# Pooled attention and an affine MLP: the order of batch 0's heads, one load for half of w_ch1, and batch 1's v summed by four tokens a partition

## The chip, the cores and the metric

The kernel runs on one core of a Trainium2 chip. A core has five engines with a program each: TensorE (PE, the matrix unit; PEld is its weight load), VectorE (DVE), ScalarE (ACT), GpSimd (POOL) and SyncE (SP). They wait for each other by semaphores. PE reads SBUF and writes PSUM; the DMA engines move data between the chip's memory and SBUF. The metric is the device time of one execution, in microseconds (us).

## The reference

q, k and v are 8 batches of 8 heads of 576 tokens by 64 numbers. Keys and values are averaged over groups of 8 tokens, so each head has 72 pooled ones. Attention's output, put together to 8 x 576 x 512, goes through an MLP with a token mix and a channel mix:

```python
k_p = k.reshape(B, H, Sp, pool, D).mean(axis=3)          # pool = 8, Sp = 72
v_p = v.reshape(B, H, Sp, pool, D).mean(axis=3)
attn = softmax(scale * q @ k_p^T)
x = (attn @ v_p), heads side by side                     # 8 x 576 x 512
a1 = alpha1 * x + beta1
u = x + lam * einsum('ts,bsd->btd', w_tok, a1)
a2 = alpha2 * u + beta2
out = u + lam * (maximum(a2 @ w_ch1, 0) @ w_ch2)         # 512 -> 2048 -> 512
```

## The kernel before

All work is written out by hand in one order; each engine runs its own instructions in that order, so an instruction that waits holds up everything behind it on its engine. The tokens of two batches make 9 chunks of 128 (4 of each, and one that holds the last 64 of both). Four chunks are a block, and there are nine blocks. Three pieces follow each other.

**The prologue** (lines 189 to 748) loads batch 0, makes constants, runs batch 0's attention and token mix and starts the MLP of block 0. Per head or head group:

- `att_F` (L367, L372) transposes q on PE and copies it from PSUM; `att_K` (L404, L410, L420) pools the keys of four heads by matmuls against a pooling matrix; `att_S` (L454, L457, L459) makes a head's scores and ACT takes their exponential into `ET`; `first_V` (L430, L432, L435) pools four heads' values on PE, four matmuls with `pool_v` (128 tokens) and two with `pool_vr` (32), and DVE copies them into `vp1_pool`, one copy for two heads.
- `att_AV` (L518, L522) multiplies `ET` by the values; DVE takes the reciprocal of the sums and scales (L524, L526). `att_X` (L540) and `rest_X` (L533) multiply by lam and alpha1 into `xs`, on DVE or GpSimd. `spread_al1` (L285, L286) spreads alpha1 over the partitions, 256 columns a call.
- `setup_wtok` (L300, L303) transposes one of five strips of w_tok, PE and an ACT copy; `setup_rowsum` (L312, L314) sums it over its tokens, for beta1. `setup_bias` (L348, L350) makes a quarter of the hidden bias from beta2 and the matching quarter of w_ch1.
- `mix_T` (L572, L576, L579) is the token mix of a chunk, five matmuls of 512 columns; `mix_uT` (L593, L595) transposes its result into `u_fm`.
- `keep_warm` (L563) is a matmul of 512 columns whose result nobody reads.

**The loads** that matter are issued by GpSimd, and so move in one queue in the order of issue: batch 0, w_tok, `load_w1(0)` and `load_w1(1)` (the four w_ch1 quarters are tiles of their own, `w1_of` picks the 128 columns of hidden chunk j), q and k of batch 1, `load_w1(2)`, v of batch 1 (`load_v`, 72 partitions, one group of 8 tokens a partition), `load_w1(3)`, and four quarters of w_ch2.

**The blocks** (lines 796 to 830): block n runs 64 `mlp_A` matmuls (L609, ACT's bias and relu L614) and 64 `mlp_B` matmuls (L643, DVE L649 and L650), with the attention and mix of batch n+1 in between. Every item has a place, a number; the list is sorted by it, and `mlp_A(n, j)` has place j, `mlp_B` 16 to 31. For batch 1 (`first`), q is transposed on PE, and `att_V` (L442, L444) sums a pair of heads' v over 8 tokens by three DVE additions. `att_S4` (L474, L481) makes four heads' scores, whose exponentials (L503) are placed one by one. Tiles named `gp` share six PSUM buffers, those named `ch` two.

Of the kernel before, what the change touches and what calls it, by code (L numbers as in the profile page):

```python
# [7 lines left out]
FP = mybir.dt.float32  # L8
F16 = mybir.dt.float16
BF = mybir.dt.bfloat16  # L10
AF = mybir.ActivationFunctionType
ALU = mybir.AluOpType
AX = mybir.AxisListType

P = 128
SPG = 72
# [7 lines left out]
def kernel(  # L24
# [18 lines left out]
    nc = tc.nc  # L43
# [21 lines left out]
    st1 = {}  # L65
# [30 lines left out]
    def load_v16(b, parts=(0, 1, 2)):  # L96
# [9 lines left out]
        for part in parts:  # L106
# [4 lines left out]
            else:  # L111
# [2 lines left out]
                    out=main[:, 4 * u:4 * u + 4].rearrange("p h c d -> p h (c d)"),  # L114
                    in_=rows(v, b, u))

    def load_rem(b, queue=nc.sync, behind=None):

        raw = work.tile([P, 2, 2, 2, D], FP, tag="rem_raw", bufs=2, name="rem_raw")
        if behind is not None:  # L120
            behind.memset(raw[:, :, :, 0, 0:1], 0.0)
        for i, src in enumerate((q, k)):
            for h in range(2):
                (nc.scalar if h and not b else queue).dma_start(
                    out=raw[:, i, h].rearrange("p c d -> p (c d)"),
                    in_=src[b, h::2, 512:576, :].rearrange("a (i c) d -> i a (c d)", c=2))
        st1[b]["rem_raw"] = raw

    def load_v(b, u, parts=(0, 1), behind=None, queue=nc.sync):

        if parts[0] != 1:
            st1[b]["v"][u] = work.tile([SPG, 4, 8, D], FP, tag="v_u", bufs=2, name="v_u")
        v_u = st1[b]["v"][u]
        if behind is not None:
            for rows_ in (slice(0, 64), slice(64, SPG)):
                behind.memset(v_u[rows_, 0, 0, 0:1], 0.0)  # L136
        for part in parts:
            g0, g1 = ((0, 64), (64, SPG), (0, SPG))[part]
            queue.dma_start(
                out=v_u[g0:g1].rearrange("g h p d -> g h (p d)"),  # L140
                in_=v[b, 4 * u:4 * u + 4, 8 * g0:8 * g1].rearrange("h (g p) d -> g h (p d)", p=8))

# [113 lines left out]
    def bias_row(i):  # L256
        p0 = 64 - 64 * i
        nc.vector.tensor_tensor(out=xs_pool[i][p0:p0 + 1, 4, :], in0=vecs[p0:p0 + 1, 1],
                                in1=vecs[p0:p0 + 1, 0], op=ALU.mult)
# [21 lines left out]
    def spread_al1(half):  # L281

        ps = gp("ps_bc")[:, 0:256]
        cols = slice(256 * half, 256 * half + 256)
        nc.tensor.matmul(out=ps, lhsT=ones_row, rhs=vecs[0:1, 2, cols])  # L285
        nc.vector.tensor_tensor(out=lamal_bc[:, cols], in0=lam_bc[:, cols], in1=ps, op=ALU.mult)  # L286
# [32 lines left out]
        nc.sync.dma_start(out=wtT[0:1, 5, 0:S], in_=wtT[64:65, 4, 0:S])  # L319


    w1 = [const.tile([P, 4, 512], BF, tag=f"w1_{g}", name=f"w1_{g}") for g in range(4)]
    w2 = [const.tile([P, 4, DM], BF, tag=f"w2_{g}", name=f"w2_{g}") for g in range(4)]

    def w1_of(cc, j):
        return w1[j // 4].rearrange("p c (m i) -> p c i m", i=4)[:, cc, j % 4, :]

    def load_w1(g):
        nc.gpsimd.dma_start(
            out=w1[g],  # L330
            in_=moe_w_ch1[:, 512 * g:512 * g + 512].rearrange("(cc p) j -> p cc j", p=P))

    def load_w2(g):
        nc.gpsimd.dma_start(
# [88 lines left out]
    def first_V(b, u, copy=nc.vector.tensor_copy):  # L423

        main, rest = st1[b]["v"]
        ps_v = gp("ps_v")
        vp = ps_v[0:SPG, 0:4 * D]
        heads = slice(4 * u, 4 * u + 4)
        for c in range(4):
            nc.tensor.matmul(out=vp, lhsT=pool_v, rhs=main[:, heads, c], start=(c == 0), stop=False)  # L430
        for c in range(2):
            nc.tensor.matmul(out=vp, lhsT=pool_vr, rhs=rest[:, heads, c], start=False,  # L432
                             stop=(c == 1))
        for r in range(2):
            copy(out=vp1_pool[2 * u + r][:, :, 0:64],  # L435
                 in_=vp[:, 128 * r:128 * r + 128].rearrange("p (h d) -> p h d", h=2))
# [122 lines left out]
    def keep_warm(count):  # L559

        ps = psB.tile([P, DM], FP, tag="ch", bufs=2, name="ps_warm")
        for _ in range(count):
            nc.tensor.matmul(out=ps, lhsT=warm[:, 0:P], rhs=warm)  # L563
# [93 lines left out]


    new_batch(1)
    for g in range(2):  # L660
        load_w1(g)
    load_q_bf(1, 0)
    load_q_bf(1, 1)
    for u in range(2):
# [10 lines left out]
    keep_warm(1)  # L675
    double_k(0)
    att_K(0, 0, None)
    bias_row(0)
    keep_warm(1)
    att_S(0, 0)  # L680
    att_S(0, 1)
    first_V(0, 0)
# [1 line left out]
    double_k(1)  # L684
    att_AV(0, 0)
    att_S(0, 3)
    keep_warm(1)
    att_K(0, 1, None)
    att_AV(0, 1)
    att_F(0, 2)  # L690
    att_F(0, 3, nc.vector.tensor_copy)
    spread_al1(0)
    att_X(0, 0, 2, nc.gpsimd, False)
    att_S(0, 4)
    att_AV(0, 2)
    spread_al1(1)
    att_S(0, 5)
    keep_warm(1)
    first_V(0, 1)
    keep_warm(1)  # L700
    att_AV(0, 3)
    att_X(0, 2, 4, nc.gpsimd, False)
    load_al2(nc.vector)
    att_S(0, 6)
    keep_warm(1)
    setup_vectors()
    att_AV(0, 4)
    keep_warm(2)
    att_S(0, 7)
    keep_warm(1)  # L710
    att_AV(0, 5)
    load_rem(1, behind=nc.vector)
    att_X(0, 4, 6, nc.gpsimd, False)
    setup_wtok(0, nc.scalar.copy)
    setup_wtok(1, nc.scalar.copy)
    att_AV(0, 6)
    setup_rowsum(0)
    att_AV(0, 7)
    setup_wtok(2, nc.scalar.copy)
    setup_rowsum(1)  # L720
    setup_bias(0)
    setup_wtok(3, nc.scalar.copy)
    att_X(0, 6, 8, nc.vector, False)
    rest_X(0, 0, H)
    load_w1(2)
    for u in range(2):
        load_v(1, u, (2,), queue=nc.gpsimd)
    mix_T(0, 0, nc.gpsimd)
    setup_rowsum(2)
    mix_T(0, 1)  # L730
    setup_rowsum(3)
    load_w1(3)
    load_w2(0)
    mix_T(0, 2, nc.gpsimd)
    load_w2(1)
    mix_uT((0, 0))
    mix_T(0, 3)
    mix_uT((0, 1))
    setup_wtok(4, nc.scalar.copy)
    setup_bias(1)  # L740
    mlp_A(0, 0, 0, 256)
    mlp_A(0, 1, 0, 256)
    mix_uT((0, 2))
    mlp_A(0, 2, 0, 256)
    mix_uT((0, 3))
    mlp_A(0, 3, 0, 256)
# [4 lines left out]
    def attention(b):  # L751


        first = b == 1
        todo = []
        if first:
            for hp in range(4):
                todo.append((2.6 + 0.9 * hp, lambda hp=hp: att_F(b, hp)))
            todo.append((3.5, lambda: cast_rem(b, nc.gpsimd)))
            for u in range(2):  # L760
                todo.append((3.65 + 0.1 * u, lambda u=u: load_w2(2 + u)))
            todo.append((7.4, lambda: att_Frem(b, nc.scalar.copy)))
        if b < B - 1:
            at = 28.5 if first else 10.0
            todo.append((at, lambda: att_F(b + 1, 0)))
            todo.append((at + 0.1, lambda: att_F(b + 1, 2)))
            at = 26.6 if first else 25.5
            todo.append((at - 1.0, lambda: cast_rem(b + 1, nc.gpsimd)))
            todo.append((at, lambda: att_Frem(b + 1)))
        for u in range(2):  # L770
            todo.append((3.6 + 0.1 * u if first else -0.9 + 1.2 * u,
                         lambda u=u: sum_k(b, u, nc.gpsimd)))
            todo.append((6.4 + 2.2 * u if first else 4.1 + 2.0 * u,
                         lambda u=u: att_K(b, u, nc.vector.tensor_copy)))
        for u in range(2):
            at = (9.0 if first else 6.3, 13.6)[u]
            todo.append((at, lambda u=u: att_S4(b, u)))
            for k, dt in enumerate((0.1, 0.1, 0.1, 0.7, 1.7, 1.75) if u else (0.1, 0.1, 0.1, 1.1, 2.1, 3.1)):
                todo.append((at + dt, lambda u=u, k=k: st1[b]["exp", u](k)))
            for i, dt in enumerate((2.9, 3.4, 4.6, 5.1) if u else (5.7, 6.2, 2.9, 3.4)):  # L780
                h = 4 * u + i
                todo.append((at + dt, lambda h=h: att_AV(b, h)))
                if i % 2:
                    eng = nc.gpsimd if h == 5 else nc.vector
                    todo.append((at + dt + 0.1, lambda h=h, eng=eng: att_X(b, h - 1, h + 1, eng)))
        for i, hp in enumerate((1, 0, 2, 3) if first else range(4)):
            todo.append(((6.6, 8.7, 10.0, 12.6)[i] if first else 0.2 + 2.0 * hp, lambda hp=hp: att_V(b, hp)))
        for c in range(5):
            at = 21.0 + 1.3 * c
            if c < 4 or b % 2:  # L790
                todo.append((at, lambda c=c: mix_T(b, c)))
                key = (b, c) if c < 4 else (b - 1, 4)
                todo.append((at + 1.8, lambda key=key: mix_uT(key)))
        return todo

    for n in range(NBLK):
# [2 lines left out]
            todo.append((j, lambda j=j: mlp_A(n, j)))  # L799
        for m in range(4):  # L800
            for part in range(4):
                at = 16 + 4 * m + part
                todo.append((at, lambda m=m, part=part: mlp_B(n, m, part)))
        if n == 0:
            todo.append((4.5, lambda: bias_row(1)))
# [55 lines left out]
```

The softmax here doesn't subtract the row's maximum and nothing guards it: scores larger than these inputs give would overflow.

## Time and profile before

| what | value |
|---|---|
| time, median of 3 | 346.69 us (346.46 to 346.94) |
| span of the profiled run | 343.8 us |
| PE busy in 0 to 20 us | 17.95 us |
| PE busy in 20 to 40 us | 19.16 us |
| PE busy in 40 to 60 us | 19.93 us |
| mlp_A L609: busy, mean of one | 133.3 us, 374 ns |
| mlp_B L643: busy, mean of one | 130.9 us, 379 ns |
| keep_warm L563: count, mean of one | 16, 505 ns |
| att_V's first additions L442, 72x512 and 72x256 | 681 ns, 420 ns |
| first_V's copies L435 | 282 ns |

Matmuls overlap in the pipeline: a mean of 379 ns for 512 columns is from start to end of one, while two starts are some 0.22 us apart. Busy time is the union. So a PE that is busy all the time isn't necessarily at its peak; what it waits for shows as idle with a releaser, and in the chain of work that ended last. A DMA issue (DMA_DIRECT2D) on GpSimd is short; the transfer behind it ends when it has landed, which the view of DMA issues lists as the time from issue to landing.

### The profile page before, as it was taken

The numbers are of one execution on the slowest core, as the hardware profiler recorded it, in microseconds if no ns is written. First come the engines' busy times: TensorE is split into PE (matmuls) and PEld (weight loads), VectorE is DVE, ScalarE is ACT, GpSimd is POOL, SyncE is SP. The second block draws the span as 40 slices with busy tenths as digits, with TensorE's granted clock in tenths as the row PEclk, the third lists the DMA queues.
The fourth block names the chain that finished last, engine by engine and source line by source line (L and its number), as shares of the span: only waits on it lengthen the run. The fifth ranks groups of instructions, "written<-read, shape, count | busy, mean of one in ns | idle before, by whom it ended". The sixth has DMA issues, their size and how long they took to land.

```text
span 343.8 us, 5902 instructions
## 1 busy us (share of the span) xinstructions
PE 337.1 (98%) x2221; PEld 177.4 (52%) x2221; DVE 224.7 (65%) x476; ACT 146.9 (43%) x277; POOL 90.2 (26%) x105
## 2 busy tenths in 40 slices
PE   8999999999999999999999999999999999999995
PEld 3667654455445544555445544554455445545544
DVE  6664579985787667866867598768675881037511
ACT  3655980068205830385028500880089006604700
POOL 8768507201144012701170117002600200000000
PEclk9999999999999999999999999999999999999999
DMA  8999999968678907794479437982810132011012
GB/s 123 184 222 287 215 202 248 188 139 130 161 210 172 194 2 192 150 225 54 129 200 213 65 110 179 204 131 63 241 41 1 48 76 78 0 61 62 2 54 68
DMA packets 66654, 45.77 MB, mean 133 GB/s; under 512 B 34457, under 2 KB 57373, under 8 KB 66626
## 3 DMA queue, kind: packets, MB, share of 16 engines
q1 hardware_dynamic: 51716, 32.73, 40.2%
q0 software_dynamic: 14448, 12.40, 22.6%
q8 instruction: 17, 0.28, 0.3%
q10 hardware_dynamic: 462, 0.27, 0.3%
q14 instruction: 11, 0.09, 0.1%
HBM read 38.30 MB, written 9.44 MB: 139 GB/s over the span
## 4 chain that ended last, share of the span: by engine, by line
PE 95%; DMA 2%; ACT 1%; DVE 1%; issue 0%; ACTq 0%; POOLq 0%
PE ps_h L609 36%; PE ps_ch L643 35%; PE ps_tok L572 11%; PE ps_s L474 2%; PE ps_av L518 2%; DMA q_bf<-in_q_dram 2%; PE ps_ch L632 1%; PE ps_kp L404 1%; PE ps_warm L563 1%; PE ps_q L367 1%; PE ps_sc L454 1%; PE ps_r L481 1%; PE ps_av L522 1%; PE ps_bias L348 0%; PE ps_bc L285 0%
## 5 line engine op out<-in xcount | busy, mean ns | idle before, releaser
L614 ACT ACTIVATE Hj<-ps_h,bias_cols 128x512 bf16<-128x512 f32 x144 | 98.3, 689 | 164.4 <-PE ps_h L609 163.1
L609 PE MATMUL ps_h<-u_fm,w 128*128 128x512 bf16 (+1 forms) x592 | 133.3, 374 | 0.2 <-ACT u_fm L595 0.2
L643 PE MATMUL ps_ch<-w,Hj 128*128 128x512 bf16 x560 | 130.9, 379 | 0.0
L609 PEld LDWEIGHTS <-w 128*128 128x128 bf16 x592 | 63.8, 114 | 51.7 <-issue 3.0
L643 PEld LDWEIGHTS <-Hj 128*128 128x128 bf16 x560 | 52.9, 98 | 61.6 <-issue 1.6
L572 PE MATMUL ps_tok<-xs,wtT 128*128 128x512 bf16 (+3 forms) x200 | 44.9, 380 | 0.3 <-DVE xs L540 0.3
L649 DVE TENSOR_TENSOR ps_ch<-lam_bc,ps_ch 128x512 f32<-128x512 f32 x32 | 22.2, 693 | 33.3 <-PE ps_ch L643 33.0
L540 POOL TENSOR_TENSOR xs<-x_tm,lamal_bc 128x512 bf16<-128x512 f32 x10 | 12.7, 1269 | 112.5 <-DVE x_tm L526 110.4
L576 DVE TENSOR_TENSOR u_sb<-x_tm,ps_tok 128x512 f32<-128x512 f32 (+1 forms) x40 | 27.4, 684 | 10.6 <-PE ps_tok L572 10.5
L524 DVE RECIPROCAL rec<-ps_av 128x5 f32<-128x5 f32 x64 | 12.2, 191 | 32.5 <-PE ps_av L522 32.4
L526 DVE TENSOR_TENSOR x_tm<-ps_av,rec 128x320 f32<-128x320 f32 x64 | 31.5, 492 | 2.7
L650 DVE TENSOR_TENSOR u_sb<-u_sb,ps_ch 128x512 f32<-128x512 f32 x35 | 24.0, 687 | 13.6 <-PE ps_ch L643 12.5
L503 ACT ACTIVATE ET<-ps_s 72x512 f16<-72x512 f32 x56 | 32.3, 592 | 0.0
L442 DVE TENSOR_TENSOR v_u<-v_u 72x512 f32<-72x512 f32 (+1 forms) x56 | 30.8, 550 | 1.0
L572 PEld LDWEIGHTS <-wtT 128*128 128x128 bf16 (+3 forms) x200 | 17.4, 100 | 21.3 <-issue 1.7
L579 DVE TENSOR_TENSOR u_bf<-u_sb,al_bc 128x512 bf16<-128x512 f32 x34 | 26.7, 785 | 1.7 <-DMA u_fm<-u_bf 0.6
L162 POOL TENSOR_TENSOR k_raw<-k_raw 128x512 f32<-128x512 f32 x14 | 18.3, 1310 | 9.1 <-DMA k_raw<-in_k_dram 6.5
L164 POOL TENSOR_TENSOR k_bf<-k_raw 128x512 bf16<-128x512 f32 x14 | 18.4, 1318 | 1.1
L518 PEld LDWEIGHTS <-ET 72*128 72x128 f16 x256 | 14.1, 97 | 8.7 <-DVE vp L435 0.2
L79 POOL DMA_DIRECT2D q_bf<-in_q_dram x16 | 12.6, 788 | 16.7 <-DVE v_u L136 15.2
L540 DVE TENSOR_TENSOR xs<-x_tm,lamal_bc 128x512 bf16<-128x512 f32 x22 | 15.4, 701 | 0.7
L518 PE MATMUL ps_av<-vp,ET 72*128 72x66 f16 x256 | 15.8, 193 | 0.0
(121 smaller groups left out, 214.9 us busy)
## 6 DMA issues: line engine op xcount, KB each, us to landing
out_dram<-u_sb SPq DMA_DIRECT2D x32, 256.0 KB
k_raw<-in_k_dram SPq DMA_DIRECT2D x12, 512.0 KB
v_u<-in_v_dram SPq DMA_DIRECT2D x12, 512.0 KB
q_bf<-in_q_dram POOLq DMA_DIRECT2D x16, 256.0 KB, 6.6
w<-in_moe_w_ch_dram POOLq DMA_DIRECT2D x8, 512.0 KB, 14.6
v_u<-in_v_dram POOLq DMA_DIRECT2D x2, 576.0 KB, 15.1
k_raw<-in_k_dram POOLq DMA_DIRECT2D x2, 512.0 KB, 15.9
rem_raw<-in_q_dram SPq DMA_DIRECT2D x15, 64.0 KB
```

The source lines that it names most:

```text
L442: nc.vector.tensor_tensor(out=t[:, :, 0:n], in0=t[:, :, 0:n], in1=t[:, :, n:2 * n], op=ALU.add)
L503: nc.scalar.activation(out=o, in_=i, func=AF.Exp, bias=0.0, scale=0.125)
L518: nc.tensor.matmul(out=av[:, odd + c, :], lhsT=ET[:, m0:m0 + 128], rhs=vp1[:, hh, :])
L526: nc.vector.tensor_tensor(out=x[:, 1 - odd:6 - odd, dd:dd + D], in0=av[:, :, 0:64], in1=rec.unsqueeze(2).to_broadcast((P, 5, D)), op=ALU.mult)
L540: eng.tensor_tensor(out=xs[:, 0:4, cols], in0=x[:, 1:5, cols], in1=lamal_bc[:, cols].unsqueeze(1).to_broadcast((P, 4, D * (h1 - h0))), op= ...
L572: nc.tensor.matmul(out=ps_tok[p0:p1], lhsT=wtT[0:kk, at, P * c:P * c + p1 - p0], rhs=xs_pool[i][0:kk, sc, :], start=(sc == 0), stop=(sc == 4))
L576: nc.vector.tensor_tensor(out=s["u"][p0:p1, :], in0=x[p0:p1, 1 + c if c < 4 else 5 - 5 * i, :], in1=ps_tok[p0:p1, 0:DM], op=ALU.add)
L579: eng.tensor_tensor(out=s["u_bf"], in0=s["u"], in1=al2_bc, op=ALU.mult)
L609: nc.tensor.matmul(out=ps_h[:, t0:t1], lhsT=w1_of(cc, j), rhs=u_fm[n][:, cc, t0:t1], start=(cc == 0), stop=(cc == 3))
L614: nc.scalar.activation(out=t, in_=ps_h, func=AF.Relu, bias=bias_cols[:, j:j + 1], scale=1.0)
L643: nc.tensor.matmul(out=ps, lhsT=Hj[n, j][:, 128 * m:128 * m + 128], rhs=w2[j // 4][:, j % 4, :], start=(j == 0), stop=(j == NJ - 1))
L650: nc.vector.tensor_tensor(out=u, in0=u, in1=ps, op=ALU.add)
```

## The change

It does six things.

- In the prologue, the scores, value mixes and set-up steps stand in another order: heads 1's mix ahead of the second key pooling, the scores of heads 5 and 6 back to back, three of the row sums ahead of the first mix and the fourth ahead of the second; 13 instead of 16 keep_warm matmuls; both key copies of the second group on ACT; six heads' `rest_X` on GpSimd.
- w_ch1 comes in three loads: half of it in the first, then a quarter each. The aim is fewer and longer pieces.
- v of batch 1 is loaded as fp32 into 128 partitions, four tokens each, and 32 partitions of two tokens for the last 64 (`load_v32`).
- DVE adds those four (two) tokens to one f16 number (`sum_v`), and `first_V` finishes the pooling on PE with one matmul each against `pool_v` and `pool_vr`; `att_V` is no longer used for batch 1.
- In block 0, batch 1's `att_K` and the mixes of heads 2 and 3 get later places.
- In block 0, `mlp_B` of chunks 0 and 1 alternate by parts, so that each quarter of w_ch2 is used for both before the next is wanted.

```diff
+    def load_v32(b):
+        main = work.tile([P, H, 4, D], FP, tag="v_u", bufs=2, name="v_main")
+        rest = work.tile([32, H, 2, D], FP, tag="v_u", bufs=2, name="v_rest")
+        nc.gpsimd.dma_start(out=main..., in_=v[b, :, 0:512, :].rearrange("h (p c) d -> p h (c d)", c=4))
+        nc.gpsimd.dma_start(out=rest..., in_=v[b, :, 512:576, :].rearrange("h (p c) d -> p h (c d)", c=2))
...
+    def sum_v(b, u):
+        if u == 2:
+            nc.vector.tensor_tensor(out=vr[:, :, 0], in0=rest[:, :, 0], in1=rest[:, :, 1], op=ALU.add)
+            return
+        m = main[:, 4 * u:4 * u + 4]
+        nc.vector.tensor_tensor(out=m[:, :, 0:2], in0=m[:, :, 0:2], in1=m[:, :, 2:4], op=ALU.add)
+        nc.vector.tensor_tensor(out=vs[:, 4 * u:4 * u + 4, 0], in0=m[:, :, 0], in1=m[:, :, 1], op=ALU.add)
...
-    w1 = [const.tile([P, 4, 512], BF, tag=f"w1_{g}", name=f"w1_{g}") for g in range(4)]
+    w1_at = (0, 2, 3, 4)
+    w1 = [const.tile([P, 4, 512 * (w1_at[i + 1] - w1_at[i])], BF, ...) for i in range(3)]
...
     (first_V)
+        n, nr = (1, 1) if b else (4, 2)
-        for c in range(4):
+        for c in range(n):
             nc.tensor.matmul(out=vp, lhsT=pool_v, rhs=main[:, heads, c], start=(c == 0), stop=False)
...
-    for g in range(2):
-        load_w1(g)
+    load_w1(0)
...
     att_K(0, 0, None)
+    spread_al1(0)
     bias_row(0)
-    keep_warm(1)
     att_S(0, 0)
...
     att_S(0, 3)
-    keep_warm(1)
-    att_K(0, 1, None)
     att_AV(0, 1)
-    att_F(0, 2)
-    att_F(0, 3, nc.vector.tensor_copy)
-    spread_al1(0)
+    att_K(0, 1, nc.scalar.copy)
+    att_F(0, 2, nc.vector.tensor_copy)
+    att_F(0, 3)
+    att_AV(0, 2)
     att_X(0, 0, 2, nc.gpsimd, False)
     att_S(0, 4)
-    (att_AV 2, spread_al1(1), att_S 5, warm, first_V(0, 1), warm)
     att_AV(0, 3)
     att_X(0, 2, 4, nc.gpsimd, False)
+    first_V(0, 1)
     load_al2(nc.vector)
+    att_S(0, 5)
     att_S(0, 6)
-    (warm, setup_vectors())
     att_AV(0, 4)
-    (warm x2)
+    spread_al1(1)
+    att_AV(0, 5)
+    att_X(0, 4, 6, nc.gpsimd, False)
     att_S(0, 7)
     keep_warm(1)
+    att_AV(0, 6)
+    setup_vectors()
     load_rem(1, behind=nc.vector)
+    keep_warm(1)
     setup_wtok(0, nc.scalar.copy)
+    att_AV(0, 7)
     setup_wtok(1, nc.scalar.copy)
+    keep_warm(2)
     setup_rowsum(0)
     setup_wtok(2, nc.scalar.copy)
+    rest_X(0, 0, 6, nc.gpsimd)
+    load_w1(1)
     setup_rowsum(1)
     setup_bias(0)
     setup_wtok(3, nc.scalar.copy)
+    att_X(0, 6, 8)
+    setup_rowsum(2)
+    keep_warm(1)
     mix_T(0, 0, nc.gpsimd)
+    setup_rowsum(3)
+    load_v32(1)
     mix_T(0, 1)
     mix_T(0, 2, nc.gpsimd)
+    load_w1(2)
     load_w2(0)
     mix_uT((0, 0))
     mix_T(0, 3)
     mix_uT((0, 1))
+    load_w2(1)
...
     (attention(1), in block 0)
-            todo.append((6.4 + 2.2 * u if first else 4.1 + 2.0 * u, ... att_K(b, u, ...)))
+            todo.append((7.0 + 2.3 * u if first else 4.1 + 2.0 * u, ... att_K(b, u, ...)))
...
-            for i, dt in enumerate((2.9, 3.4, 4.6, 5.1) if u else (5.7, 6.2, 2.9, 3.4)):
+            early = (5.7, 6.2, 3.5, 4.0) if first else (5.7, 6.2, 2.9, 3.4)
...
+        if first:
+            for i, u in enumerate((0, 2, 1)):
+                todo.append((10.4 + 0.1 * i, lambda u=u: sum_v(b, u)))
+            for u in range(2):
+                todo.append((12.0 + 0.9 * u, lambda u=u: first_V(b, u)))
...
     (mlp_B)
-                at = 16 + 4 * m + part
+                at = 16 + (2 * part + m if n == 0 and m < 2 else 4 * m + part)
```

Lines in brackets name a place in the code or several removed calls.

## The prediction

> **What bounds the kernel now.** I read the page from the top: busy shares, the 40 slices, then the chain of work that ended last.
>
> ```profile
> PE 337.1 (98%) x2221; PEld 177.4 (52%) x2221; DVE 224.7 (65%) x476; ACT 146.9 (43%) x277; POOL 90.2 (26%) x105
> ...
> DMA  8999999968678907794479437982810132011012
> ...
> PE 95%; DMA 2%; ACT 1%; DVE 1%; issue 0%; ACTq 0%; POOLq 0%
> ```
>
> TensorE (PE) is busy 98% of the span and carries 95% of the chain, so every PE instruction added or removed, and every wait of PE, moves the end one for one. The second row (40 slices of 8.6 us) has DMA at 90% and more from slice 2 to slice 8, to 69 us, and thinner afterwards. So a second bound is near in that stretch: the loads, which come one behind the other on GpSimd's queue. From 69.6 us (block 1) on nothing is edited, and PE has no idle there worth a name; the edits count by when block 1 can start.
>
> Next the chain around the start of the mixes, in order of time (start us, us, what):
>
> ```profile
> 20.25 0.70 ACT wtT L303
> 20.95 0.04 issue
> 20.99 0.44 PE ps_rs L312 x5
> 21.43 0.12 PE ps_av L518 x4
> 21.55 0.04 PE ps_av L522
> 21.60 0.02 issue
> 21.62 0.21 DVE rec L524
> 21.83 0.02 issue
> 21.85 0.50 DVE x_tm L526
> 22.35 0.02 issue
> 22.38 0.70 DVE xs L540
> 23.08 0.14 issue
> 23.21 1.24 PE ps_tok L572 x5
> ```
>
> Here PE isn't the bound: it waits for ACT's copy of a transposed w_tok tile, and the first mix (L572) waits for the last head's division and scaling on DVE. The PE timeline of the same stretch (start, us, engine, line) gives the order on PE:
>
> ```profile
> 21.70 0.39 PE L312 MATMUL ps_rs<-wtT,ones_bf 128*128 128x128 bf16 x4
> 21.93 0.22 PE L312 MATMUL ps_rs<-wtT,ones_lo 128*128 128x128 bf16 x1
> 21.98 0.67 PE L348 MATMUL ps_bias<-b2c_bf,w 128*128 128x1 bf16 x16
> 22.51 0.45 PE L300 MATMUL ps_w<-identity_bf,wt_bf 128*128 128x128 bf16 x5
> 23.21 1.24 PE L572 MATMUL ps_tok<-xs,wtT 128*128 128x512 bf16 x5 [0.25 <-DVE xs L540]
> ```
>
> L348 at 21.98 is setup_bias(0), which reads w_ch1's first quarter. When did that land? GpSimd's timeline has the issues, and the view of DMA issues, restricted to 9.4 to 10.1 us and to 10.2 to 10.8 us, has the time from issue to landing (the last column):
>
> ```profile
> 9.35 1.59 POOL L329 DMA_DIRECT2D w<-in_moe_w_ch_dram  x2
> ```
>
> ```profile
> w<-in_moe_w_ch_dram POOLq DMA_DIRECT2D x1, 512.0 KB, 11.5
> ```
>
> ```profile
> w<-in_moe_w_ch_dram POOLq DMA_DIRECT2D x1, 512.0 KB, 14.1
> ```
>
> The first quarter landed at 9.35+11.5 = 20.85 us, 1.1 us before setup_bias(0) read it; the second, issued at 10.1, at 24.2 us, needed only at 28.9 by setup_bias(1). The same view puts w_tok's last part, issued at 8.8, at 17.9 us: the weights queue behind it.
>
> **What the Trainium skill says.** *DMA: Bandwidth & Descriptors*, "Why a DMA increments its semaphore by 16 and not by 1": a transfer runs on up to 16 engines that finish independently, and "only the full 16 means 'all data landed'". So a reader of any part of a load waits for the whole. The trace agrees as far as it goes: the two quarters, two loads, landed 3.4 us apart. *TensorEngine Tiling (Array Packing)*, "Key Properties": changing the tiling mode drains TensorE. The trace shows such a step: from the 128-row L430 to the 32-row L432 starts are 0.203 us apart instead of 256/2.4 GHz = 0.107, and 0.19 to 0.20 back, so 0.09 to 0.10 us at each change. *TensorE: Matmul & The Clock Gate*, "What's actually happening": after an idle window of about 3.4 us the array runs at half rate. The trace has the cold rate at the start alone: 0.427 us between L563 matmuls before 8.4 us, 0.22 later.
>
> **The change, part by part.**
>
> *Prologue up to setup_bias(0).* Eight keep_warm matmuls of 0.22 us stood between 9.2 us and setup_bias(0); now four do: 0.88 us less. spread_al1(0), 0.62 us at 14.1, moves to 9.4, into the wait of the first scores for kpT (0.4 us idle in front of 9.87): about 0.4 us less. The wait of 0.54 us ahead of the first row sum (20.45 to 20.99) gets a head's mix, five transposes and two warm matmuls in it. A few tenths go back, because F3's copy and both kpT copies now stand on ACT ahead of the exponentials and because V's second half lands at 14.8, just when first_V(0,1) is reached. In sum PE gets to setup_bias(0) about 1.6 us earlier, at 20.4.
>
> *The load.* There PE meets the new load. Half of w_ch1 is one transfer, so setup_bias(0) waits for both quarters. In the packet records a quarter is 512 packets of 1024 bytes (written) at 98 ns, over 16 engines 3.14 us, 6.27 us for two. The new load has 512 packets of 2048 bytes, which the trace doesn't show: at the most 196 ns (twice the small one, nothing saved), at the least 162 ns (the rate of w_ch2's 4096-byte packets, 324 ns). A line through 98 and 324 ns gives 173 ns, 5.54 us, 0.73 us saved. All loads ahead of it keep their order, so it lands at 24.2-0.73 = **23.5 us** (ends 23.1 and 24.2; the small loads of rem and alpha2 now come up to 2.4 us earlier and may add some tenths). PE stands still from 20.4 to 23.5. Everything behind it on PE in program order waits: wtok(3), two row sums, all mixes, the whole of block 0.
>
> From there: weight load 0.1, bias 0.53, wtok(3) 0.28, row sum 0.28, warm 0.22, mix 0 1.08, row sum 0.28; mix 1 starts at 26.27. In before it started at 24.57 with one row sum (0.28) still to come. **Net +1.4 us.** All prologue savings are swallowed by this wait, and so are the moved DVE, ACT and GpSimd operations (rest_X on GpSimd, kpT and qT copies): they finish while PE waits.
>
> *Between the mixes and block 0.* One transpose moves ahead of mlp_A(0,1). The last u_fm copy still has only mlp_A(0,3)'s 0.44 us to hide under, so the 0.4 us idle ahead of 32.07 stays: nothing. GpSimd now issues two V loads between u_bf(0) and u_bf(2); by my count u_bf(2) is ready at about 31.1, and PE wants it at 31.2: nothing, 0.3 us at worst.
>
> *V of batch 1.* DVE loses 4 x (0.681+0.420+0.289) = 5.6 us (L442, L444 by form) and gets 2 x (0.681+0.420) + 0.681 + 4 x 0.282 (L435) = 4.0 us. DVE isn't the bound; worth nothing as such. PE gets two first_V of two matmuls: 0.107+0.107 and two changes of row count, 0.40 us each: **+0.8 us**, with nothing to hide it. Then a new wait: head 2's mix now stands right behind first_V(1,0) (places 12.0 and 12.5, no mlp_A between) and needs the second of its two PSUM copies. In the prologue the same path took from 17.36 (PE free of first_V(0,1)) to 17.99 (second copy done): **+0.6 us**; sum_v, 2.9 us on DVE behind kp's copy, is done at about the same time as PE's first_V, so it may add a little. Behind this mix stand first_V(1,1) and mlp_A(13). In exchange the 0.26 us for which the second head group's scores (46.27) waited for ACT's exponentials is covered: **-0.26**. V as 128 partitions uses the engines more evenly than 72 and lands 1 to 2 us earlier; nobody waited for it.
>
> *mlp_B's interleaving.* Each w_ch2 quarter is now wanted two to three places later or at the same one. No PE wait stood there before (last quarter landed at 51.7): nothing.
>
> Sum: +1.4 +0.8 +0.6 -0.26 = +2.6 us, so 346.69+2.6 = **349.3 us**.
>
> **The rivals.** *Faster:* the half lands by 20.4 after all, and the two copies are done in time. Then bias 0.53, wtok(3), row sum, warm bring mix 0 to 21.7 and mix 1 to 23.1; less the row sum already done, that is 1.75 us ahead of before; with +0.8 -0.26 it is -1.2 us, 345.5. For it: PE's order was thinned out by 0.88 us. Against it: with a landing at 20.4 the 1 MiB would have to move in 2.5 us, where the quarters took 2.95 and 3.4 each. *No change:* the load is early but V's path costs as counted: -1.75+1.18 = -0.6, 346.1. *Slower still:* the idle of 3.1 us, or more if the small loads delay the half, trips the clock gate; one window of 3.4 us at half rate costs 1.7 us: 351.0. Against it: the idle is shorter than the page's window, and windows seldom line up.
>
> **How the numbers follow.** Forecast 0.70 (349.3, from 348.0 to 350.3 by the ends of landing, copy wait and POOL), faster 0.11 (345.5), no change 0.08 (346.1), slower still 0.11 (351.0). A rise of 0.2% begins at 347.4. Range 346.9 to 351.2: both slower cases, and the foot towards no change. Chances: faster 0.12, same 0.07, slower 0.81.
>
> **What would show it.** PE idle in front of L348's first group (of the changed file) for about 3 us, released by the DMA of w, at about 23.5; mix 1 starting at 26.3; four more 256-column ps_v matmuls in block 0, and about 0.6 us without PE between them and the next ps_av; block 1 starting at about 72.2 instead of 69.6. Wrong if the first L348 starts before 22 us, or if block 1 starts before 70 us.

## The result and the profile after

The changed kernel took 350.37 us (median of four runs, 349.69 to 352.2), the kernel before 346.57 us beside it (346.3 to 346.94): a ratio of 1.0117, 95% interval 1.0073 to 1.0161, so 1.2% slower. The forecast was 349.3 us in a range of 346.9 to 351.2. The direction and the first step are as forecast; the time is about a microsecond over it. The profile below is of the slowest of the four runs (352.2 us), so it shows the loss at its largest. Ratios here and below leave out a run more than 1.5% above the fastest of its kernel (one of bias_late, one of split_oldv); medians and ranges keep it.

First the page of the changed kernel: busy times and instruction counts, the granted TensorE clock in 40 slices (tenths of full speed), and the shares of the chain that ended last.

```profile
PE 337.7 (96%) x2183; PEld 179.1 (51%) x2222; DVE 222.2 (63%) x472; ACT 147.2 (42%) x278; POOL 90.3 (26%) x105
...
PEclk9987999999999999999999999999999999999999
...
PE 88%; DMA 6%; POOL 2%; DVE 2%; issue 2%; ACT 0%; SPq 0%; POOLq 0%; DVEq 0%
```

PE is still on the path almost throughout, but the chain now holds 6% of DMA instead of 2%, and the third and fourth slice (17.5 to 35 us) had a clock of 0.8 and 0.7. The kernel before has 9 in every slice. PE's count of 2183, against 2221 before, is no saving: the weight loads (PEld) are 2222 against 2221, so 39 matmul records are missing from this trace, and PE's busy time of 337.7 us isn't exact either.

The chain of the changed kernel around the start of the mixes (start us, us, what):

```profile
9.34 14.58 DMA w<-in_moe_w_ch_dram
23.92 0.05 issue
23.97 0.70 PE ps_bias L374 x16
24.66 0.56 PE ps_w L321 x5
25.23 0.55 PE ps_rs L333 x5
25.77 0.20 issue
25.98 2.34 PE ps_tok L599 x5
28.32 0.53 PE ps_rs L333 x5
28.85 3.00 PE ps_tok L599 x10
```

Before, the chain here went through ACT's copy of w_tok and DVE's scaling of the last head. Now it goes straight back to the issue of the half of w_ch1 at 9.34 us, which lands 14.58 us later, at 23.92. L374 is setup_bias(0). The view of what PE waited for between 20 and 26 us (total us, times, longest) has one wait of weight:

```profile
PE ps_bias L374 <- DMA w<-in_moe_w_ch_dram: 2.6, 1, 2.6
```

The wait is the forecast one, nearly at the forecast moment (23.92 against 23.5). But the lines after it are not what the prediction counted: five matmuls of a mix (L599, 512 columns) take 2.34 us instead of 1.08, which is 427 ns from one start to the next. The table of windows shows it for two stretches of this kernel (window, length, then busy us and instructions of PE, PEld, DVE, ACT and POOL, granted clock, DMA share, GB/s):

```profile
20.00:24.00 4.00, 1.40 (x18) 0.99 (x17) 1.98 (x3) 2.09 (x5) 2.01 (x3) 0.95 1.09 196
24.00:31.00 7.00, 6.78 (x43) 3.94 (x45) 0.88 (x2) 1.37 (x4) 1.86 (x2) 0.54 1.20 288
```

The second stretch in the kernel before:

```profile
24.00:31.00 7.00, 7.00 (x73) 4.86 (x71) 4.94 (x7) 2.39 (x7) 5.10 (x7) 1.00 1.20 290
```

PE is busy in both, but with 43 instructions at a clock of 0.54 where it did 73 at 1.00. The clock records put the half rate from 23.6 to 30.4 us, 6.8 us long. The Trainium skill, *TensorE: Matmul & The Clock Gate*, "What's actually happening", has a free-running window of 3413 ns behind this. The trace agrees: the 6.83 us at half rate are two of these, the 13.65 us at full rate ahead of them four. The page puts the drop after an idle window. Here PE was busy 1.40 of the 4.00 us up to 24.0, and 1.18 of the 3.41 us up to the drop (20.19 to 23.60), so in this profile a window that was partly busy seems to have counted as idle.

The sum for this profile is thus:

| place | before | after | difference |
|---|---|---|---|
| block 0 starts (first mlp_A), us | 29.48 | 34.15 | +4.67 |
| block 0 itself, us | 39.96 | 41.15 | +1.19 |
| block 1 starts, us | 69.44 | 75.30 | +5.86 |
| span of the profiled run, us | 343.8 | 350.5 | +6.7 |

Another 0.5 us went to one wait for a transposed u_fm at about 182 us, which the kernel before doesn't have. Of the +4.67, the 6.4 us of PE work done at half rate (23.97 to 30.4) account for about 3.2 us; the rest, about 1.5, is the forecast +1.4.

The four runs had mean clocks of 0.990, 0.995, 1.0 and 0.994. Span times the missing share gives an estimate of what the half rate cost each: 3.4, 1.7, 0 and 2.1 us. Without it their median would be about 348.9 us, so the half rate is enough for the microsecond over the forecast.

Block 0's +1.19 us is V's new way. PE and DVE around first_V(1,0) and the mix of head 2 behind it, from the changed kernel's timelines (start, us, engine, line, and in brackets a wait and its releaser):

```profile
49.65 0.27 PE L457 MATMUL ps_v<-vs,pool_v 128*72 128x256 f16 x1
49.86 0.29 PE L459 MATMUL ps_v<-vr,pool_vr 32*72 32x256 f16 x1
50.73 0.30 PE L545 MATMUL ps_av<-vp,ET 72*128 72x66 f16 x4 [0.58 <-DVE vp L462]
```

```profile
49.45 0.43 DVE L138 TENSOR_TENSOR vs<-v_main 128x256 f16<-128x256 f32 x1
50.19 0.48 DVE L462 CAST vp<-ps_v 72x128 f16<-72x128 f32 x2 [0.31 <-PE ps_v L459]
```

PE has put out the pooled V at about 50.15, DVE copies it in two pieces up to 50.67, and only then can head 2's mix go. Summed over block 0, from one start on PE to the next: first_V costs 0.89 us, the wait 0.62, the scores give back 0.34 (1.77 to 1.43) because their wait for the exponentials is covered. 0.89 + 0.62 - 0.34 = 1.17.

### The profile page after: what moved, and what is told of

Same layout as the page of the kernel before. It is cut to its first block, busy times and chain, and to the rows that moved or that the text cites. A ratio compares the mean times of both kernels' runs of the same rounds, so it can differ in the third digit from the quotient of the medians.

```text
span 350.5 us, 5859 instructions
## 1 busy us (share of the span) xinstructions
PE 337.7 (96%) x2183; PEld 179.1 (51%) x2222; DVE 222.2 (63%) x472; ACT 147.2 (42%) x278; POOL 90.3 (26%) x105
## 4 chain that ended last, share of the span: by engine, by line
PE 88%; DMA 6%; POOL 2%; DVE 2%; issue 2%; ACT 0%; SPq 0%; POOLq 0%; DVEq 0%
PE ps_h L636 35%; PE ps_ch L670 32%; PE ps_tok L599 11%; DMA w<-in_moe_w_ch_dram 4%; PE ps_s L501 2%; PE ps_av L545 2%; DMA u_fm<-u_bf 2%; PE ps_ch L659 1%; PE ps_bias L374 1%; PE ps_r L508 1%; PE ps_kp L430 0%; PE ps_av L549 0%; POOL v L113 0%; DVE ps_ch L676 0%; DVE u_sb L603 0%
## 5 line engine op out<-in xcount | busy, mean ns | idle before, releaser
L670 PE MATMUL ps_ch<-w,Hj 128*128 128x512 bf16 x543 | 128.5, 379 | 0.9 <-issue 0.5
L599 PE MATMUL ps_tok<-xs,wtT 128*128 128x512 bf16 (+3 forms) x200 | 46.7, 392 | 0.5 <-PE ps_rs L333 0.2
L599 PEld LDWEIGHTS <-wtT 128*128 128x128 bf16 (+3 forms) x200 | 18.1, 103 | 22.5 <-issue 3.9
L469 DVE TENSOR_TENSOR v_u<-v_u 72x512 f32<-72x512 f32 (+1 forms) x48 | 27.4, 571 | 0.8
L606 DVE TENSOR_TENSOR u_bf<-u_sb,al_bc 128x512 bf16<-128x512 f32 x34 | 25.4, 746 | 1.7 <-DMA u_fm<-u_bf 0.5
```

The source lines that it names most:

```text
L469: nc.vector.tensor_tensor(out=t[:, :, 0:n], in0=t[:, :, 0:n], in1=t[:, :, n:2 * n], op=ALU.add)
L599: nc.tensor.matmul(out=ps_tok[p0:p1], lhsT=wtT[0:kk, at, P * c:P * c + p1 - p0], rhs=xs_pool[i][0:kk, sc, :], start=(sc == 0), stop=(sc == 4))
L606: eng.tensor_tensor(out=s["u_bf"], in0=s["u"], in1=al2_bc, op=ALU.mult)
L670: nc.tensor.matmul(out=ps, lhsT=Hj[n, j][:, 128 * m:128 * m + 128], rhs=w2[j // 4][:, j % 4, :], start=(j == 0), stop=(j == NJ - 1))
```

## The experiments

The question was what the wait for the half costs, what V costs, and why the mixes ran at half rate. The theory: (1) the merged load makes PE stand still at setup_bias(0); (2) V's way adds 1.2 us on PE; (3) the standstill lets the clock fall. Rivals: the loss lies in the new order and not in the load; the clock falls by itself, whatever PE does. Ratios are to the kernel before, run beside (medians of 346.49, 346.43 and 346.19 us in the three sets).

**The load in quarters again** (split_w1), all else as changed:

```diff
-    w1_at = (0, 2, 3, 4)
+    w1_at = (0, 1, 2, 3, 4)
...
     load_w1(0)
+    load_w1(1)
...
     rest_X(0, 0, 6, nc.gpsimd)
-    load_w1(1)
+    load_w1(2)
...
     mix_T(0, 2, nc.gpsimd)
-    load_w1(2)
+    load_w1(3)
```

> The changed kernel with w_ch1 in four quarter loads again; all else as changed. Theory (the wait of setup_bias(0) for the half load carries most of the loss): the first quarter lands at about 20.5 to 20.9 us, PE is there at 21.2 and doesn't wait, no matmul runs at half rate after that, and what is left is V's cost on PE (+1.3 us by the working of the prediction) less what the order saves (0.7): 347.1 us. Rival (the new order or V's path is what costs): 349.5 or more, as in the changed kernel's fastest runs. Second rival (the slower quarter loads delay later w_ch1 or v and the wait moves there): 348 to 349, with a DMA wait of PE in block 0.

Measured: 347.01 us (345.03 to 349.78, 22 runs), 1.0019 [0.9999, 1.0039]. Its chain (start us, us, what):

```profile
22.52 0.32 PE ps_rs L333 x5
22.83 0.51 PE ps_bias L374 x16
...
24.14 1.08 PE ps_tok L599 x5
```

setup_bias(0) runs right behind the row sum, without a wait (the first quarter landed at 21.06), a mix takes 1.08 us, and block 0 starts at 29.96. Most of the loss is gone with the merged load (forecast 347.1 us), and the interval takes in no change at all. Block 0, from 29.96 to 71.11, is 41.15 us: V's +1.19 is unchanged.

**The half load kept, its first reader moved** (bias_late):

```diff
-    setup_bias(0)
     setup_wtok(3, nc.scalar.copy)
...
     setup_wtok(4, nc.scalar.copy)
+    setup_bias(0)
     setup_bias(1)
```

> The changed kernel, half load kept, with setup_bias(0) moved from behind the second row sum to just ahead of setup_bias(1), where the half has long landed. Theory: the load itself is harmless, only its first reader on PE stands too early; the wait of 2.6 us goes, mix 0 starts at about 22.2 instead of 26.0, no half rate: 347.1 us. Rival (DMA as such is the bound and PE will wait for something else, such as v or the third quarter): 348.5 or more. Rival (order and V cost): 349.5 or more.

Measured: 348.45 us (345.87 to 353.38, 22 runs), 1.0043 [1.0021, 1.0065]. Nine of the runs lie at 345.9 to 346.8 and most others at 348 to 351, so the median sits between two groups and above the 347.1 us expected; the lower group is where the kernel before lies. The profiled one (348.9 us) has no wait for w; its chain ahead of the mixes is:

```profile
21.87 0.29 PE ps_w L321 x5
...
22.18 1.30 ACT wtT L324 x2
...
23.50 0.26 ACT wtT L335
...
23.78 0.70 ACT wtT L324
24.48 0.04 issue
24.52 0.44 PE ps_rs L333 x5
```

In this run the load is off the path, and PE still comes to the mixes late, because it came to w_tok's transposes late: the clock records show the full rate from 17.8 us only, where the kernel before has it from 8.9. So there is a second way to lose time, which no wait shows.

**The half load alone in the kernel before** (merge_only):

```diff
-    w1 = [const.tile([P, 4, 512], BF, tag=f"w1_{g}", name=f"w1_{g}") for g in range(4)]
+    w1_at = (0, 2, 3, 4)
+    w1 = [const.tile([P, 4, 512 * (w1_at[i + 1] - w1_at[i])], BF, tag=f"w1_{i}", name=f"w1_{i}")
+          for i in range(3)]
...
-    for g in range(2):
-        load_w1(g)
+    load_w1(0)
...
```

> The kernel before with one edit, the half load of w_ch1 in place of the first two quarters. Theory: setup_bias(0), reached at 21.98 us, waits until 23.9; mix 0 starts at about 24.85 instead of 23.2: +1.6 us, 348.2 us; the idle of 1.9 us is too short to slow the clock. Rival (the larger load is harmless or gains by its longer packets): 346.0 to 346.7. Rival (the merge alone makes all of the loss, half rate with it): 350.

Measured: 346.87 us (345.74 to 349.8, 22 runs), 1.0016 [1.0001, 1.0032]. The forecast was 1.3 us too high. Its chain and its wait:

```profile
9.35 13.57 DMA w<-in_moe_w_ch_dram
22.92 0.05 issue
22.97 0.69 PE ps_bias L353 x16
23.66 0.31 PE ps_w L300 x5
23.97 1.13 PE ps_tok L577 x5
```

```profile
PE ps_bias L353 <- DMA w<-in_moe_w_ch_dram: 0.2, 1, 0.2
```

In the old order PE gets there just as the half lands. Part of that is this execution's clock: it rose at 10.67 us, where the kernel before has it at 8.95, and PE came at about 22.8 instead of 21.98. At 21.98 the wait would have been 0.9 us (an estimate, 22.92 less 21.98).

The half also lands a microsecond earlier than in the changed kernel's first profile (22.92 against 23.92). All six profiles with the half point to the small loads. In the first profile and in warm6 the 128 packets of rem move from 20.4 us on, while the half is still under way, and it lands at 23.9 to 24.0. In merge_only, bias_late, warm_fill and after_again they move from 22.8 us on, and it lands at 22.9 to 23.0. By their 96 ns each over 16 engines they take an estimated 0.8 us. They weren't moved by themselves. The merge costs little alone; it costs more with an order that brings PE and the small loads there earlier.

**Filling the wait with warm matmuls** (warm_fill with 12, warm6 with 6):

```diff
     setup_rowsum(1)
+    keep_warm(12)      # warm6: keep_warm(6)
     setup_bias(0)
```

> The changed kernel with 12 more keep_warm matmuls (12 x 0.216 = 2.6 us) right ahead of setup_bias(0): PE waits as long for the load but isn't idle. Theory (the idle trips the clock gate in some executions and that makes the difference between runs of 349.7 and 352.2): no 427 ns matmuls after 24 us, mix 1 at about 26.5 and all runs near 349.6, none above 350.2. Rival (the half rate and the spread have another cause): matmuls at 427 ns after 24 us as before, runs from 349.7 to 352.

> The changed kernel with 6 keep_warm matmuls (1.3 us) ahead of setup_bias(0), half of the longest wait seen. Theory (the drop of the clock comes from idle time): no drop at 24 us in the profile and a granted clock of 0.998 or more in every run; the time falls to 349.2 to 350.0, as the fill costs nothing where the wait was 2.6 us and at most 1.3 us where PE came late. Rival (the drop has another cause): runs with a clock of 0.995 and less stay as frequent as in after_again.

Measured: warm_fill 350.79 us (348.84 to 352.02, 6 runs), 1.0123 [1.0097, 1.015], with a mean clock of at least 0.999 in every run; warm6 350.21 us (348.54 to 351.01, 6 runs), 1.0111 [1.0088, 1.0134], with 0.995 and 0.992 in two of the six. The changed kernel had 0.990 to 0.995 in three of its first four runs. Both times miss what was expected (near 349.6, none above 350.2; 349.2 to 350.0), and so does warm6's clock. Twelve fillers went with a steady clock and bought nothing: in the profiled run PE was late again (full rate from 17.7), so the fill itself was the delay, with setup_bias(0) at 26.36 and the load landed at 22.98. With six, PE still waited 1.2 us in the profile:

```profile
PE ps_bias L374 <- DMA w<-in_moe_w_ch_dram: 1.2, 1, 1.2
```

The profiled run of warm6 had no drop behind the wait, and block 0 started at 31.31: 1.83 us later than before, where the prediction had +1.4. This is the forecast mechanism without the drop. What brings the drop isn't settled by these two. A count over all runs says more; a mean clock of 0.995 or less stands for some 3.5 us at half rate or more:

| kernel | runs with 0.995 or less |
|---|---|
| changed (both sets) | 5 of 10 |
| warm6, warm_fill | 2 of 6, 0 of 6 |
| merge_only | 3 of 22 |
| split_w1, bias_late | 0 of 22, 0 of 22 |
| split_oldv, best1 (below; no merged load) | 3 of 22, 1 of 14 |
| before, beside in the three sets | 2 of 153 |

So the drop goes with the wait, but it also comes, more rarely, where there is no merged load to wait for.

**The changed kernel once more, unedited** (after_again):

> The changed kernel itself, unedited, on the chip of this call, for its spread beside the others'. Theory (wait for the half load, and the half rate after it when the wait is long): runs from 349 to 352, median 350.4; where the profile shows PE at setup_bias(0) before 21.5 us the clock drops at about 24 us and comes back 6.8 us later; where the clock comes up late, PE is there later, waits less and there is no drop. Rival (the first four runs were unlucky): median 348 or less.

Measured: 348.76 us (347.94 to 350.15, 6 runs), 1.0084 [1.0062, 1.0107], clocks 0.995 to 1.0: lower than the 349 to 352 expected, and 2.57 us above the kernel before (346.19). Its profiled run took the other way round. The chain:

```profile
24.23 0.32 PE ps_rs L333 x5
24.55 0.51 PE ps_bias L374 x16
...
25.86 1.08 PE ps_tok L599 x5
```

The load had landed at 22.91 and nobody waited for it. PE itself came at 24.4 us: three microseconds later than in the first profile of the same kernel (21.4). The windows from 8 to 14 us say why; first this run, then the kernel before, in the columns of above:

```profile
8.00:14.00 6.00, 6.00 (x41) 3.82 (x40) 2.72 (x10) 2.86 (x8) 4.45 (x7) 1.00 1.45 201
```

```profile
8.00:14.00 6.00, 5.55 (x81) 4.08 (x79) 3.14 (x10) 4.08 (x12) 4.43 (x8) 1.00 1.40 175
```

PE is busy the whole 6 us with 41 instructions where the kernel before does 81 in 5.55. The clock column reads 1.00 in both, but this run's first clock record stands at 19.1 us; ahead of the first record the column is not evidence, the counts are. In its profiles the changed kernel has two ways to lose at setup_bias(0): PE early and the load not there (23.97), or the clock late and PE not there (24.4). Both end at nearly the same place.

**The first stretch as before** (split_early: split_w1 with two of the removed warm matmuls put back and spread_al1(0) at its old place):

```diff
     att_K(0, 0, None)
-    spread_al1(0)
     bias_row(0)
+    keep_warm(1)
     att_S(0, 0)
...
     att_S(0, 3)
+    keep_warm(1)
     att_AV(0, 1)
...
     att_F(0, 3)
+    spread_al1(0)
```

> split_w1 with the first stretch of the prologue as before: keep_warm ahead of the first scores and ahead of head 1's mix, spread_al1(0) behind att_F(0, 3). In split_w1's profile the clock became full at 14.7 us only, in bias_late's at 17.8, in before's at 8.9. Theory (the thinner early PE work lets the clock come up a window or more later in many executions, which makes the spread of 345.0 to 349.8): the clock is full by 11 us in the profile, the highest run is below 348.5 and the median 346.3 or less. Rival (when the clock comes up is chance and not in the kernel's order): median and spread as split_w1's, 347.0, 345 to 349.8.

Measured: 347.33 us (345.98 to 349.26, 22 runs), 1.0022 [1.0008, 1.0036]: the expected 346.3 was missed, and so was the bound of 348.5 (two runs lie above 349). The median isn't below split_w1's; only the spread is narrower (middle half 346.72 to 347.6 against 345.81 to 348.77). The windows line of its profiled run, the fastest of the 22:

```profile
8.00:14.00 6.00, 5.55 (x82) 4.09 (x80) 4.09 (x14) 4.17 (x13) 4.79 (x8) 1.00 1.44 199
```

82 instructions: full rate. Over all profiles, the first clock record stands at 8.0 to 10.7 us in the six whose first stretch is that of before (two of them, best2 and best3 below, with one warm matmul more), and in the eight with the new first stretch at 9.7 to 10.0 us (three) or at 14.7 to 19.1 us (five). One profile each is thin, and the edits of the stretch weren't tried apart, but no late one occurs in the old order. Of the profiled runs without the wait for the half, all of different kernels, those with a late rise took 347.3 to 351.0 us and those with an early one 345.1 to 346.0 (best2, with another wait, 347.5). So the late clock is a likely cause of the scatter, but split_early's median shows that it isn't the whole of it.

**V back on DVE** (split_oldv: split_w1 with batch 1's V and block 0's places as before; best1: the first stretch as before too):

```diff
-    load_v32(1)
+    for u in range(2):
+        load_v(1, u, (2,), queue=nc.gpsimd)
...
-                todo.append((12.0 + 0.9 * u, lambda u=u: first_V(b, u)))
+            todo.append(((6.6, 8.7, 10.0, 12.6)[i] if first else 0.2 + 2.0 * hp, lambda hp=hp: att_V(b, hp)))
...
```

> split_w1 with batch 1's v and its places in block 0 as before (load_v on GpSimd, att_V on DVE). From the first mlp_A to block 1's first: 39.96 us in before, 41.15 in the changed kernel and in all its variants so far. Theory (V on PE costs 0.8 us of matmuls and a wait of 0.77 for DVE's copies): 39.96 again, median 1.2 us below split_w1's: 345.8. Rival (mlp_B's interleaving or the order of loads makes the longer block 0): 41.15 stays, 347.0.

> Quarter loads, the first stretch of the prologue as before, batch 1's v as before; left of the change are the later order of the prologue, the row sums ahead of the mixes and mlp_B's interleaving. Theory: block 0 starts at 28.6 to 29.0 us (29.48 in before), takes 39.96, 345.5 to 346.0: faster than before by 0.2%. Rival (before's prologue was already held by something else, such as the loads of q, k and v): block 0 starts at 29.4 or later and the time is before's, 346.5.

Measured: split_oldv 347.33 us (345.05 to 351.24, 22 runs), 1.0015 [0.9998, 1.0032]; best1 346.84 us (344.75 to 349.44, 14 runs), 1.0015 [0.999, 1.0039]. Both medians miss what was expected (345.8; 345.5 to 346.0). In the profiles, block 0 did start early, at 28.42 and 28.92 us, but it took 40.52 and 40.47 us, where 39.96 had been counted on. The chain of split_oldv has the reason (SPq is the queue of the transposing loads):

```profile
56.74 0.70 DVE ps_ch L679
...
57.46 0.70 DVE u_sb L680
...
58.18 0.38 SPq L682
...
58.61 10.20 DMA u_fm<-u_bf x2
...
68.94 1.24 PE ps_h L639 x5
```

mlp_B's results leave through DVE and SyncE's queue. Alternating chunks 0 and 1 puts them there at other moments, and block 1's first u_fm transpose, behind them on that queue, comes late: PE starts block 1 0.56 us late. Counted from the first mlp_A, that first transpose was issued at 30.2 us in split_oldv and best1, at 29.3 before, and at 29.1 and 29.8 in best2 and best3 below, which put the chunks one after the other. In the changed kernel's own block 0 this wait doesn't show.

**Head 2's and 3's mixes later** (split_av: split_w1 with the mixes out of the wait for V's copies):

```diff
-            early = (5.7, 6.2, 3.5, 4.0) if first else (5.7, 6.2, 2.9, 3.4)
+            early = (5.7, 6.2, 4.1, 4.2) if first else (5.7, 6.2, 2.9, 3.4)
```

> split_w1 with the mixes of heads 2 and 3 of batch 1 behind mlp_A(13) instead of ahead of and behind it: the two copies of first_V(1, 0) have 1.3 us of PE work to hide under. Theory: the wait of 0.77 us ahead of ps_av goes and nothing takes its place: block 0 at 40.4 us, 346.3. Rival (the wait moves on to the second head group's scores or exponentials): block 0 at 40.8 or more.

Measured: 346.14 us (345.12 to 349.65, 14 runs), 1.001 [0.9984, 1.0035]. The wait of 0.62 us for V's copies is gone in the profile, as planned, but block 0 took 41.08 us and not the 40.4 expected: 0.35 us went into the wait for u_fm, by the same route, and 0.2 us back into the scores (1.65 us instead of 1.43), where the rival had put it. The median meets the expected 346.3, but not by the route behind it. The profiled run (348.6 us, a late clock) is one of the slow ones of the 14.

**What the findings add up to** (best2: best1 with mlp_B's chunks one after the other and one more warm matmul in the first stretch; best3: split_early with split_av's places, the same mlp_B and the same warm matmul):

```diff
-    keep_warm(3)
+    keep_warm(4)
...
-                at = 16 + (2 * part + m if n == 0 and m < 2 else 4 * m + part)
+                at = 16 + 4 * m + part
```

> best1 (quarter loads, first stretch and v as before) with mlp_B's parts in before's order and a fourth keep_warm in the second group of three. In best1 and split_oldv block 1 waited 0.35 to 0.56 us for the transposed u_fm, whose chain runs through DVE's work on the two chunks that mlp_B finishes late. Theory: block 0 is 39.96 us again, starts at about 28.8: 345.2 in the profile, median 346.0. Rival (the new order makes block 0 early and it then waits for u_fm or another transfer whatever mlp_B's order): block 0 at 40.3 or more and the median at before's, 346.5.

> split_early with the mixes of heads 2 and 3 behind mlp_A(13), mlp_B's parts in before's order, and a fourth keep_warm in the second group: v on PE kept, with its wait and the wait for u_fm taken away. Theory: block 0 at 40.4 us (39.96 + 0.8 of first_V - 0.26 to 0.4), start 28.8: 345.7 in the profile, median 346.5. Rival (the wait for the two copies or for u_fm stays): block 0 at 40.8 to 41.1, median 347.

Measured: best2 346.13 us (344.68 to 347.47, 22 runs), 0.9997 [0.9985, 1.0008]; best3 345.93 us (345.37 to 347.16, 14 runs), 0.9999 [0.9987, 1.0011]. Neither beats the kernel before, though both medians lie near what was expected or below. best3's waits of PE from 8 to 70 us:

```profile
PE ps_sc L481 <- ACT kpT L446: 0.3, 1, 0.3
PE ps_h L636 <- ACT u_fm L622: 0.2, 1, 0.2
PE ps_sc L481 <- DVE kpT L446: 0.2, 1, 0.2
```

All waits of weight are gone, and its block 0 takes 40.74 us from 28.80: 69.54, within 0.1 us of the kernel before (69.44). The profiled run of best2, the slowest of its 22, shows the next bound:

```profile
PE ps_h L639 <- DMA u_fm<-u_bf: 2.5, 1, 2.5
PE ps_ch L673 <- DMA w<-in_moe_w_ch_dram: 0.6, 1, 0.6
```

PE reached block 0 at 28.12 and then waited 0.6 us for w_ch2's last quarter and 2.5 us for transposes; its block 0 took 43.30 us. In this execution the earlier PE meets the loads, as the busy DMA row of the first profile hinted; how often that happens isn't shown.

## Why the prediction was right, and where it was off

- **The wait for the half load: right.** One wait of 2.6 us, released by the DMA of w (forecast 3.1), and gone in split_w1. PE came at 21.4 and not 20.4, the load at 23.92 and not 23.5, so the two errors partly cancel: the new order brought PE there 0.6 us earlier and not 1.6. The packets, which had to be interpolated, are right: 173 ns each in the trace (median), 5.6 us for the load. The 0.4 us by which the landing was missed is inside the range that was left for the small loads. Of the two profiles of the unedited changed kernel only the first has the wait. after_again's median lies 2.57 us above the kernel before, where +2.6 was forecast, but its profile got there by the late clock, so that agreement is partly luck.
- **All prologue savings swallowed: right for the changed kernel.** Without the wait it depends on the clock. split_w1's profile, with a late rise, starts block 0 at 29.96, 0.48 us behind before; split_oldv's and split_early's, with an early one, start it at 28.42 and 28.62, about a microsecond ahead.
- **Mix 1 at 26.27: mis-sized.** It was 28.64, 27.06 and 26.69 in the first profile, after_again and warm6. The step said that after the wait everything runs at its old duration. It runs so in warm6 (+1.83 us at block 0), but in the first profile 6.4 us ran at half rate. The prediction had this as "slower still" with one window and 11%; half of the changed kernel's ten runs show it, and in the first profile it lasted two windows. The argument against it, an idle shorter than the window, didn't hold: a wait of 2.6 us was enough there.
- **The late clock: not in the prediction at all.** The removed warm matmuls were counted as 0.88 us saved and never as work that may lift the clock. after_again shows three microseconds lost by it with no wait at all. It is likely to be a part of why bias_late and split_w1 scatter so widely; for the runs without a profile that isn't shown.
- **V's way +1.14 to 1.18: right.** 1.19 us measured, and 41.15 us for block 0 again in split_w1, bias_late, split_early, warm_fill and warm6 (41.32 in after_again). Its terms: first_V 0.89 (0.8), wait 0.62 (0.6), scores -0.34 (-0.26). The forecast terms add up to 1.14; the 1.18 of the "no change" rival doesn't follow from them. With them the whole sum is 2.54 us, given as 2.6. The two copies that the wait was sized by end at 17.94 in the trace and not 17.99, which changes nothing.
- **mlp_B's alternation at nothing: right for the changed kernel, not in general.** As soon as block 0's PE gets earlier, 0.35 to 0.56 us appear as a wait for u_fm (split_av, split_oldv).
- **The "faster" and "no change" rivals** needed the half by 20.4 us; it never landed before 22.9.
- **Block 1 at 72.2:** 75.3, 73.0 and 72.5 us in the first profile, after_again and warm6. Only warm6, with its six fillers, is near the forecast; the first has a half-rate stretch behind the wait, after_again one in its late start.

Open stays what sets off the drop of the clock. In the first profile it follows a window in which PE was busy 1.18 of 3.41 us; in warm6's profile the same window (20.20 to 23.61) had 2.62 and no drop followed. The drop is most frequent where the wait is, but the kernels without the merged load show it too. And it was not separated whether the removed warm matmuls or the early spread_al1(0) bring the late rise.

## What to carry to other kernels

Merging two loads makes the first reader wait for the last byte: set the landing of the whole against the moment at which the reader gets there in the new order, since the same merge cost 0.2 us of waiting in one profile of the old order (0.9 by the estimate above) and 2.6 in one of the new. Short matmuls with no other use may be holding the clock; before taking them out as savings, look for when the clock first comes up, and compare instruction counts per window and not busy shares. And where a kernel has PE, loads and transposes all within half a microsecond of each other, taking a wait off one shows the next: the sum of single savings isn't the saving.

## What the hardware showed that was not expected

- A half-rate stretch of 6.83 us followed a wait of 2.6 us, with PE busy 35% of the 3.41 us ahead of it. In the first half of that stretch PE was busy 2.82 of 3.41 us, and the full rate came back only after the second, with 3.41 of 3.41.
- The first rise of the clock came at anything from 8.0 to 19.1 us of the profiles, though PE was already busy for 6.00 of the 6 us from 8 to 14 in a late one. So PE's busy time alone doesn't say when the clock rises; what does, no run here tests.
- The half of w_ch1 (1 MiB written, in packets of 2048 bytes) took 173 ns a packet, against 98 ns for the quarters' 1024 and 324 for w_ch2's 4096.
